# Raw attention scores stored with neighbouring queries interleaved in DRAM: wider fetches, split stores

## The chip, the cores and the metric

The kernel runs on one core of a Trainium2 chip. The core has five engines with a queue each: TensorE (PE for matmuls, PEld for the weight loads that run beside them), VectorE (DVE), ScalarE (ACT), GpSimd (POOL) and SyncE (SP, which here issues all transfers), and 16 DMA engines that move data between DRAM and the core's SBUF. The metric is the device time of one execution in microseconds, the median of several runs. All data are 32-bit floats.

## The reference

Attention with mixing over the heads before and after the softmax, followed by a gated layer without a nonlinearity:

```python
# q, k, v: [8 batches, 12 heads, 448, 64]; w_pre, w_post: [12, 12]
scores = scale * np.matmul(q, k.transpose(0, 1, 3, 2))
scores = np.einsum('bhij,hg->bgij', scores, w_pre)
scores = scores - np.max(scores, axis=-1, keepdims=True)
attn = np.exp(scores)
attn = attn / (np.sum(attn, axis=-1, keepdims=True) + 1e-09)
attn = np.einsum('bhij,hg->bgij', attn, w_post)
attn_out = np.matmul(attn, v)
...
x = attn_out.transpose(0, 2, 1, 3).reshape(8 * 448, 768)
h = (x @ w1) * (x @ w2) @ w3        # w1, w2: [768, 1024], w3: [1024, 1024]
return h @ w_out                    # [1024, 768]
```

## The kernel before

**Raw scores.** `qk` (L167) makes the raw scores of two heads (a head pair `p`) for a chunk `c` of 128 queries: eight matmuls into two PSUM tiles `psq` (one per head), two ScalarE copies into a stage tile `st` of 128 queries x 2 heads x 448 keys (L180, L181), and a store of `st` to the DRAM tensor `raw_d[b]` of 448 queries x 12 heads x 448 keys. The last chunk has 64 queries only, so two head pairs share its `st`, which leaves in two stores (L186); the others leave in one (L189). A batch has 21 such units: 18 of chunks 0 to 2 and three of chunk 3. `st` has two buffers per pool. The store is not issued at once: `qk` returns it, and the step loop puts it on the list `later` for the next step.

**Mixing over heads.** TensorE contracts over partitions, so for the mixing the heads must lie on partitions. `fetch` (L196) reads `raw_d` back by blocks of ten queries (45 blocks a batch, the last with eight): five queries x 12 heads are 60 rows, the two halves `s` of a block stand at partitions 0 and 64 of the tile `r`, and the two blocks `c` of a pair lie side by side along the free dimension. Two blocks of one batch and of full width come in two transfers, one per half (L203); other pairs (across two batches, or with the eight-query block) in four (L210). `r` has two buffers. `mix` (L215) multiplies by the pre-mixing weights into `psm` (L221); `largest` (L224) takes the maximum, `exp` (L231) the exponentials `e` and their sums, `scale` (L240) folds the reciprocal sums into the post-mixing weights `w2`, and `post` (L251) mixes again and transposes into the PSUM tiles `pso`. `put` (L273) copies `pso` into `mt` (L275; the eight-query block in two copies, L278), where the queries of a group of 15 blocks stand in order. `av` (L293) multiplies `mt` by `v` for a whole group.

**The gated layer** runs on TensorE between these parts as a background: first the product w3 @ w_out (L361), then batches 0 and 1 one by one (L523, L554), then the other six in pairs, in a scheme with seven products (L704). Its weights come in units `wu` from DRAM (L394); from batch 2 on the attention results pass through DRAM as `x_d` and are read back as `x` (L620).

**Order.** Everything is issued by a hand-written loop of steps (from L893 on, N = 360 blocks and six more); step `n` handles block pair `m = n // 2`, with different work in odd and even steps. In an even step SyncE gets first the fetch of the pair two ahead, which must wait until the mixing of the pair that held the buffer is done. Then come, by `do_later`, the weight units due, the list `later` (stores of raw scores and others), the operands `x`, and then the next `kq` (queries and keys of a head pair, L158). SyncE works through its queue in order: a transfer that waits holds up those behind it. The raw scores of batch 1 begin at step 11, beside those of batch 0; those of batch `b` > 1 are spread over the 45 steps before that batch's own blocks begin.

Of the kernel before, what the change touches and what calls it, by code (L numbers as in the profile page):

```python
# [6 lines left out]
F32 = mybir.dt.float32  # L7
# [8 lines left out]
B, H, S, D = 8, 12, 448, 64  # L16
DM, FF = 768, 1024
HP = H // 2
IB = 10
GI = H * IB  # L20
NB = -(-S // IB)
QT, NJ = 128, 4
GB = 15
NG = NB // GB
KF, K1 = FF // 128, DM // 128
IH = IB // 2
HK = H * IH
PP = 64
JB = S // PP
SETS = NB * B // 2  # L30
FIRST = 48
# [19 lines left out]
class Kernel:  # L51
# [115 lines left out]
    def qk(self, b, p, c, banks):  # L167


        nc = self.nc  # L170
        ps = [self.bank(i, f"psq{b}_{p}_{c}_{s}")[:, :S] for s, i in enumerate(banks)]
        for z, (t, q, k) in enumerate(self.parts(b, p, c)):
            for s in range(2):
                rows = slice(s * D, (s + 1) * D)
                nc.tensor.matmul(ps[s][z * PP:(z + 1) * PP], t[rows, q:q + PP], t[rows, k:k + S], start=True, stop=True)  # L175
        if b == c == 0:
            st = self.sz[:, 2 * p:2 * p + 2]
        else:
            st = (self.qp if b == 0 and p % 2 else self.kp).tile([128, 2, S], F32, tag="st", name=f"st{b}_{p}_{c}", bufs=2)
        nc.scalar.copy(st[:, 0], ps[0])  # L180
        (nc.vector.tensor_copy if b == c == 0 else nc.scalar.copy)(st[:, 1], ps[1])  # L181
        raw = self.raw_d[b]
        if c == 3:
            def store():
                for z in range(2):
                    nc.sync.dma_start(raw[3 * QT:, 2 * (p + z) - 2:2 * (p + z)], st[z * PP:(z + 1) * PP])  # L186
            return store
        n = QT if b or c else FIRST
        return lambda: nc.sync.dma_start(raw[c * QT:c * QT + n, 2 * p:2 * p + 2], st[:n])  # L189


# [4 lines left out]
    def fetch(self, m):  # L196
        r = self.rp.tile([128, 2, S], F32, tag="r", name=f"r{m}", bufs=2)
        self.rs[m] = r
        b, t = divmod(2 * m, NB)
        if t + 1 < NB and self.width(2 * m + 1) == IB:  # L200
            src = self.raw_d[b][t * IB:(t + 2) * IB].rearrange("(c s i) h j -> s (i h) c j", c=2, s=2)
            for s in range(2):
                self.nc.sync.dma_start(r[s * PP:s * PP + HK], src[s])  # L203
            return
        for c in range(2):
            b, t = divmod(2 * m + c, NB)
            for s in range(2):
                k = self.half(2 * m + c, s)
                src = self.raw_d[b][t * IB + s * IH:t * IB + s * IH + k].rearrange("i h j -> (i h) j")
                self.nc.sync.dma_start(r[s * PP:s * PP + H * k, c], src)  # L210

    def half(self, n, s):
        return min(IH, self.width(n) - s * IH)

    def mix(self, m):  # L215
        nc, r = self.nc, self.rs.pop(m)
# [34 lines left out]
    def post(self, m):  # L251
        nc, w2s = self.nc, self.w2s.pop(m)
        if any(b in (4, 5) for b, _ in self.ends):
            self.do_ends()
        for s, e in enumerate(self.es.pop(m)[0]):
            for j in range(JB):
                a, z = divmod(j, 2) if j < JB - 1 else (NJ - 1, s)
                at = (2 * a + s) * HK
                for c in range(2):
                    k = slice(c * PP, c * PP + HK)  # L260
                    nc.tensor.matmul(self.pso[c][z * PP:(z + 1) * PP, at:at + HK], e[k, j * PP:(j + 1) * PP], w2s[k, s],  # L261
                                     start=True, stop=True)
        for c in range(2):
            n = 2 * m + c
            w, (b, t) = self.width(n), divmod(n, NB)
            a, u = divmod(t, GB)
            if u == 0:
                self.mt[b, a] = self.mp.tile([128, NJ, H, GB * IB], F32, tag="mt", name=f"mt{b}_{a}")
            src = self.pso[c][:, :NJ * 2 * HK].rearrange("p (j s g i) -> p j s g i", j=NJ, s=2, g=H)
            dst = self.mt[b, a][:, :, :, u * IB:u * IB + w]  # L270
            self.ends.append((4 + c, lambda dst=dst, src=src, w=w: self.put(dst, src, w)))

    def put(self, dst, src, w):  # L273
        if w == IB:
            self.nc.scalar.copy(dst.rearrange("p j g (s i) -> p j s g i", s=2), src)  # L275
        else:
            for s, k in ((0, IH), (1, w - IH)):
                self.nc.scalar.copy(dst[:, :, :, s * IH:s * IH + k], src[:, :, s, :, :k])  # L278
# [465 lines left out]
    def run(self):  # L744
        nc, tc = self.nc, self.tc
# [5 lines left out]
        self.jobs, self.ys, self.pairs = [], {}, False  # L751
        dp = self.pool("dram", 1, space=DRAM)
        self.ps = self.pool("ps", 1, space=PSUM)
        self.raw_d = [dp.tile([S, H, S], F32, name=f"raw{b}_d") for b in range(B)]
        self.w_d = [dp.tile([KF, 128, k, 2, 128], F32, name=f"w{i}_d") for i, k in enumerate((K1, K1, KF))]
        self.x_d = [dp.tile([2, 128, K1 // 2, S], F32, name=f"x{b}_d") for b in range(B)]
        self.s_d = [{m: dp.tile([c, 128, k * 256], F32, name=f"s{i}_{m}_d") for m in (3, 5, 6, 7)}
# [22 lines left out]
        w = self.kp.tile([128, 2, S], F32, tag="st", name="wpre_s", bufs=2)[:, 0, :PP]  # L780
# [35 lines left out]
        for b in range(1, B):  # L816
            first, per = (11, 28 / 21) if b == 1 else ((b - 1) * NB - 6, NB / 21)
            units = [(b, p, c) for g in range(0, HP, 2) for p, c in [*itertools.product((g, g + 1), range(3)), (g + 1, 3)]]
            for i, (b, p, c) in enumerate(units):
                n = int(first + i * per) | (b > 1)  # L820
# [3 lines left out]
        for b in range(B):  # L824
            for a in range(NG):
                for g in range(HP):
                    n = (b * NB + (a + 1) * GB + 3) | 1
# [65 lines left out]
        for n in range(N + 6):  # L893
# [34 lines left out]
            m, odd = divmod(n, 2)  # L928
# [10 lines left out]
            p, pieces = self.n_made - 1 if fold_pieces else 2 * KF + 3 * KF, None  # L939
            if avs.get(n):  # L940
                pass
            elif fold_pieces:
                f = (self.n_made - 1 - 2 * KF) // 3
# [68 lines left out]
def words(w):  # L1012

    import numpy as np
    return np.ascontiguousarray(w).view(np.int64)


def layouts(inputs):
    import numpy as np
    q, k, v = inputs["q"], inputs["k"], inputs["v"]  # L1020
    qt = q.transpose(0, 1, 3, 2).reshape(B, HP, 2, D, S)
    kt = k.transpose(0, 1, 3, 2).reshape(B, HP, 2 * D, S)
    kq = np.ascontiguousarray(np.stack([qt.reshape(B, HP, 2 * D, S), kt], axis=3))
    q0 = qt[0].reshape(HP, 2 * D, S)
    kq0 = np.ascontiguousarray(np.concatenate([q0[:, :, :QT], kt[0], q0[:, :, QT:]], axis=2))
    vv = np.concatenate([v, v[:, :, (NJ - 1) * 128:]], axis=2)
    vv = vv.reshape(B, HP, 2, NJ, 128, D).transpose(0, 1, 4, 3, 2, 5).reshape(B, HP, 128, NJ, 128)
    wpre = np.zeros((128, PP), np.float32)
    wpost = np.zeros((128, HK), np.float32)
    for s in range(2):  # L1030
        for i in range(IH):
            rows = slice(s * PP + i * H, s * PP + (i + 1) * H)
            wpre[rows, i * H:(i + 1) * H] = inputs["w_pre"]
            wpost[rows, i::IH] = inputs["w_post"]
    return {
        "kq": kq, "kq0": kq0, "v": np.ascontiguousarray(vv), "wpre": wpre, "wpost": wpost,
        "w1": words(inputs["moe_w1"]), "w2": words(inputs["moe_w2"]),
        "w3t": words(inputs["moe_w3"].T), "wo": words(inputs["moe_w_out"]),
    }
# [16 lines left out]
```

## Time and profile before

| | |
|---|---|
| median of three runs | 1437.4 us (1436.35 to 1438.15) |
| the profiled execution | 1441.87 us, of which its span is 1439.9 us |
| TensorE busy | 1386.1 us (96%), weight loads 1056.7 us |
| ScalarE, VectorE, GpSimd busy | 833.3, 742.8, 622.0 us |
| read from DRAM, written to it | 279.77 MB, 134.09 MB |

The profile's page gives busy times, the span in 40 slices, the DMA queues, a chain of work followed back from the last instruction, the costliest groups of instructions (by line, engine, tiles and shape, with busy time, mean duration and what ended the idle time before them) and the DMA issues with their median time to landing. Further views tell who waited for whom, list instructions or transfers of a stretch of time, and tabulate busy times by stretches. A matmul's end is modelled, so a busy TensorE is not one at its peak.

### The profile page before, as it was taken

How to read it: one execution, taken by the hardware profiler on the slowest of the kernel's cores; microseconds unless marked ns; L12 is line 12 of the kernel's file. 1: busy time of each engine (PE TensorE's matmuls, PEld its weight loads, DVE VectorE, ACT ScalarE, POOL GpSimd, SP SyncE). 2: the span in 40 equal slices, each digit the busy share in tenths (PEclk: the TensorE clock that was granted, in tenths of full speed). 3: DMA queues.
4: the chain of work that ended last, by engine and by line, in shares of the span. 5: the costliest groups of instructions: out<-in, count | busy, mean ns of one | idle time of the engine just before them, and what ended most of it. 6: DMA issues, size and time to landing. Idle time of an engine off the chain costs nothing.

```text
span 1439.9 us, 45779 instructions
## 1 busy us (share of the span) xinstructions
PE 1386.1 (96%) x18684; PEld 1056.7 (73%) x18684; DVE 742.8 (52%) x1497; ACT 833.3 (58%) x1952; POOL 622.0 (43%) x754
## 2 busy tenths in 40 slices
PE   5879999999999999999999999999999999999998
PEld 2357786766677767776777777777777777889988
DVE  5957566767644545432344435334444456345563
ACT  4866666767756756665655556556556445432231
POOL 1423233444324544532345345434335436457693
PEclk8989999999999999999999999999999999999999
DMA  8998789999999999999889988799979757698775
GB/s 283 366 319 277 237 266 321 325 312 305 313 280 356 368 357 318 380 348 333 286 266 290 315 289 265 247 316 332 300 229 301 248 174 224 196 327 268 239 234 171
DMA packets 203761, 416.87 MB, mean 290 GB/s; under 512 B 20528, under 2 KB 120112, under 8 KB 203472
## 3 DMA queue, kind: packets, MB, share of 16 engines
q1 hardware_dynamic: 203552, 413.94, 87.5%
q8 instruction: 149, 2.44, 0.7%
q14 instruction: 60, 0.49, 0.1%
HBM read 279.77 MB, written 134.09 MB: 287 GB/s over the span
## 4 chain that ended last, share of the span: by engine, by line
PE 81%; DMA 9%; DVE 5%; ACT 2%; issue 1%; SPq 0%; POOL 0%; DVEq 0%; POOLq 0%; ACTq 0%
PE e L704 20%; PE psa L302 11%; PE pso L261 10%; PE psm L221 8%; PE psq L175 7%; PE eg L523 6%; PE psf L361 4%; PE eo L554 4%; PE e2o L704 4%; PE e3o L704 4%; DMA wu<-w_d 3%; PE e1o L704 3%; DMA raw_d<-st 2%; DMA cs<-wo 2%; DMA r<-raw_d 1%
## 5 line engine op out<-in xcount | busy, mean ns | idle before, releaser
L248 POOL TENSOR_SCALAR w<-wpo,ri 128x60 f32<-128x60 f32 x360 | 180.3, 517 | 482.9 <-DVE ri L246 464.6
L228 DVE TENSOR_REDUCE mn<-psm 128x1 f32<-128x448 f32 x360 | 207.6, 618 | 319.1 <-PE psm L221 318.8
L275 ACT COPY mt<-pso 128x480 f32<-128x480 f32 x352 | 197.8, 621 | 183.6 <-PE pso L261 183.4
L704 PE MATMUL e<-eh,wu 128*128 128x448 f32 x1008 | 297.3, 371 | 4.4 <-DVE c L658 3.2
L236 ACT ACTIVATE e<-psm,mn 128x448 f32<-128x448 f32 x360 | 226.8, 643 | 8.3 <-DVE mn L228 8.3
L704 PEld LDWEIGHTS e<-eh,wu 128*128 128x128 f32 x1008 | 187.5, 188 | 50.9 <-issue 25.1
L221 PE MATMUL psm<-r,wsc 60*64 60x448 f32 (+1 forms) x1440 | 193.1, 552 | 20.7 <-DVE cx L124 7.8
L261 PEld LDWEIGHTS pso<-w,e 60*64 60x64 f32 x10080 | 175.3, 135 | 50.9 <-issue 42.2
L261 PE MATMUL pso<-w,e 60*64 60x60 f32 x10080 | 199.2, 224 | 0.4 <-ACT mt L275 0.3
L704 PE MATMUL e<-el,wu 128*128 128x448 f32 x504 | 186.8, 371 | 0.0
L302 PE MATMUL psa<-mt,v 128*64 128x150 f32 (+1 forms) x2304 | 158.5, 294 | 4.2 <-ACT st L180 4.2
L302 PEld LDWEIGHTS psa<-mt,v 128*64 128x64 f32 x2304 | 145.1, 138 | 20.3 <-ACT st L180 6.9
L175 PE MATMUL psq<-kq 64*64 64x448 f32 x1176 | 156.1, 542 | 4.0 <-ACT st L180 4.0
L658 DVE TENSOR_TENSOR c<-c,e 128x448 f32<-128x448 f32 x168 | 101.6, 617 | 82.5 <-PE e L704 77.9
L180 ACT COPY st<-psq 128x448 f32<-128x448 f32 x162 | 86.5, 534 | 79.7 <-ACT mt L275 34.1
L523 PE MATMUL eg<-xh,wu 128*128 128x448 f32 x384 | 118.8, 380 | 3.3 <-DMA wu<-w_d 3.3
L643 POOL TENSOR_TENSOR el<-x,eh 128x448 fp32r<-128x448 f32 x90 | 104.2, 1174 | 34.4 <-ACT eh L642 28.9
L704 PEld LDWEIGHTS e<-el,wu 128*128 128x128 f32 x504 | 94.6, 188 | 22.2 <-issue 14.1
L175 PEld LDWEIGHTS psq<-kq 64*64 64x64 f32 x1176 | 60.7, 135 | 58.1 <-issue 30.0
L523 PEld LDWEIGHTS eg<-xh,wu 128*128 128x128 f32 x384 | 71.4, 189 | 36.0 <-issue 24.7
L245 DVE TENSOR_SCALAR sa<-sm 128x2 f32<-128x2 f32 x180 | 35.2, 196 | 116.0 <-ACT e L236 115.6
L181 ACT COPY st<-psq 128x448 f32<-128x448 f32 x162 | 87.8, 542 | 0.0
(99 smaller groups left out, 2015.6 us busy)
## 6 DMA issues: line engine op xcount, KB each, us to landing
r<-raw_d SPq DMA_DIRECT2D x344, 210.0 KB, 5.4
raw_d<-st SPq DMA_DIRECT2D x138, 448.0 KB, 6.2
wu<-w_d SPq DMA_DIRECT2D x104, 384.0 KB, 6.4
wu<-s_d SPq DMA_DIRECT2D x96, 384.0 KB, 4.9
wu<-w_d SPq DMA_DIRECT2D x51, 512.0 KB, 6.2
kq<-kq SPq DMA_DIRECT2D x42, 448.0 KB, 7.1
wu<-s_d SPq DMA_DIRECT2D x36, 512.0 KB, 5.0
x<-x_d SPq DMA_DIRECT2D x72, 224.0 KB, 6.4
```

What stands on the lines that cost most here:

```text
L175: nc.tensor.matmul(ps[s][z * PP:(z + 1) * PP], t[rows, q:q + PP], t[rows, k:k + S], start=True, stop=True)
L221: nc.tensor.matmul(ps[s][c * PP:(c + 1) * PP, :S], self.wsc[k], r[k, c], start=True, stop=True)
L228: self.nc.vector.tensor_reduce(mn[:, s:s + 1], self.psm[m][s][:, :S], axis=AX.X, op=ALU.min)
L236: nc.scalar.activation(e, p[:, :S], AF.Exp, bias=mn[:, s:s + 1], scale=-1.0, accum_out=sm[:, s:s + 1])
L248: nc.gpsimd.tensor_scalar_mul(w2[:, s], self.wpo, ri[:, s:s + 1])
L261: nc.tensor.matmul(self.pso[c][z * PP:(z + 1) * PP, at:at + HK], e[k, j * PP:(j + 1) * PP], w2s[k, s], start=True, stop=True)
L275: self.nc.scalar.copy(dst.rearrange("p j g (s i) -> p j s g i", s=2), src)
L302: nc.tensor.matmul(self.psa[rows, g % 3, :W], v[:, j, rows], mt[:, j, 2 * g + s, :W], start=(j == 0), stop=(j == NJ - 1))
L523: nc.tensor.matmul(p, u[:, k % (K1 // 2), x], xs[y][:, k], start=(k == 0 and t == 0), stop=(k == K1 - 1 and t == 2))
L643: nc.gpsimd.tensor_tensor(lo, x, hi.bitcast(F32), op=ALU.subtract)
L658: nc.vector.tensor_tensor(a[out], a[to[0]], p, op=ALU.add)
L704: nc.tensor.matmul(p, w[:, k, x], ops[m, k][y], start=(k == 0 and t == 0), stop=(k == nk - 1 and t == 2))
```

## The change

For batches 1 to 7 `raw_d[b]` becomes a tensor of 224 query pairs x 12 heads x 2 x 448 keys: for each head the scores of queries 2i and 2i + 1 are neighbours. On the host the queries of each chunk are reordered, even ones first, so that partitions 0 to 63 of `st` hold the even queries of a chunk and 64 to 127 the odd ones. Each `st` leaves in two stores of 64 partitions (chunk 3: four of 32), each with two runs of 448 numbers per partition. A pair of full blocks of one group of 15 is fetched in two transfers whose 60 rows are one run of 896 numbers each; `c` is now the parity of the query and `s` the half of the twenty. Pairs that cross a group, a batch or meet the eight-query block come in four transfers, with `s` as the parity. `put` writes with a step of two so that `mt` has the queries in order as before. Batch 0 stays as it is.

```diff
@@ qk
         raw = self.raw_d[b]
+        if b:
+            n, parts = (PP // 2, ((2 * p - 2, 0), (2 * p, PP))) if c == 3 else (PP, ((2 * p, 0),))
+
+            def store():
+                for h, k in parts:
+                    for z in range(2):
+                        nc.sync.dma_start(raw[c * PP:c * PP + n, h:h + 2, z], st[k + z * n:k + (z + 1) * n])
+            return store
...
-        n = QT if b or c else FIRST
+        n = QT if c else FIRST
@@ fetch
         b, t = divmod(2 * m, NB)
-        if t + 1 < NB and self.width(2 * m + 1) == IB:
+        if self.paired(2 * m):
+            src = self.raw_d[b][t * IH:(t + 2) * IH].rearrange("(s i) h c j -> s (i h) c j", s=2)
+            for s in range(2):
+                self.nc.sync.dma_start(r[s * PP:s * PP + HK], src[s])
+            return
+        if b == 0 and t + 1 < NB and self.width(2 * m + 1) == IB:
...
-                src = self.raw_d[b][t * IB + s * IH:t * IB + s * IH + k].rearrange("i h j -> (i h) j")
+                raw = self.raw_d[b][t * IH:t * IH + k, :, s] if b else self.raw_d[b][t * IB + s * IH:t * IB + s * IH + k]
+                src = raw.rearrange("i h j -> (i h) j")
                 self.nc.sync.dma_start(r[s * PP:s * PP + H * k, c], src)
 
     def half(self, n, s):
-        return min(IH, self.width(n) - s * IH)
+        return min(IH, self.width(n) - s * IH) if n < NB else self.width(n) // 2
+
+    def paired(self, n):
+
+        t, u = n % NB, (n ^ 1) % NB
+        return n >= NB and n // NB == (n ^ 1) // NB and t // GB == u // GB and self.width(n) == self.width(n ^ 1) == IB
@@ post
-            dst = self.mt[b, a][:, :, :, u * IB:u * IB + w]
-            self.ends.append((4 + c, lambda dst=dst, src=src, w=w: self.put(dst, src, w)))
-
-    def put(self, dst, src, w):
-        if w == IB:
+            if b == 0:
+                dst = self.mt[b, a][:, :, :, u * IB:u * IB + w]
+            elif self.paired(n):
+                dst = self.mt[b, a][:, :, :, (u - c) * IB:(u - c + 2) * IB].rearrange("p j g (s i c) -> p c j s g i", s=2, c=2)[:, c]
+            else:
+                src = src[:, :, :, :, :w // 2]
+                dst = self.mt[b, a][:, :, :, u * IB:u * IB + w].rearrange("p j g (i s) -> p j s g i", s=2)
+            self.ends.append((4 + c, lambda dst=dst, src=src, w=w, b=b: self.put(dst, src, w, b)))
+
+    def put(self, dst, src, w, b):
+        if b:
+            self.nc.scalar.copy(dst, src)
+        elif w == IB:
             self.nc.scalar.copy(dst.rearrange("p j g (s i) -> p j s g i", s=2), src)
@@ run
-        self.raw_d = [dp.tile([S, H, S], F32, name=f"raw{b}_d") for b in range(B)]
+        self.raw_d = [dp.tile([S // 2, H, 2, S] if b else [S, H, S], F32, name=f"raw{b}_d") for b in range(B)]
@@ layouts
-    kq = np.ascontiguousarray(np.stack([qt.reshape(B, HP, 2 * D, S), kt], axis=3))
+    order = [c + 2 * i + z for c, n in ((0, QT), (QT, QT), (2 * QT, QT), (3 * QT, PP)) for z in range(2) for i in range(n // 2)]
+    kq = np.ascontiguousarray(np.stack([qt.reshape(B, HP, 2 * D, S)[..., order], kt], axis=3))
```

## Prediction

> **What bounds the kernel now.** I read the page first, then the table of stretches, the waits of TensorE, the chain in the stretch with the most idle time, and last the two queues of work that the change touches: SyncE's issues and the stage copies of ScalarE. From the page:
>
> ```profile
> PE 1386.1 (96%) x18684; PEld 1056.7 (73%) x18684; DVE 742.8 (52%) x1497; ACT 833.3 (58%) x1952; POOL 622.0 (43%) x754
> ...
> DMA  8998789999999999999889988799979757698775
> ...
> DMA packets 203761, 416.87 MB, mean 290 GB/s; under 512 B 20528, under 2 KB 120112, under 8 KB 203472
> ...
> q1 hardware_dynamic: 203552, 413.94, 87.5%
> ```
>
> TensorE is busy 1386.1 of 1439.9 us, so no change to transfers can win more than the other 53.8 us. But the DMA engines are almost as full. The table of stretches (us, then PE, PEld, DVE, ACT and POOL busy with counts, the granted clock, DMA share, GB/s) says where:
>
> ```profile
> 40.00:100.00 60.00, 43.94 (x631) 24.67 (x633) 46.33 (x90) 44.76 (x108) 22.45 (x28) 0.92 1.02 362
> ...
> 240.00:300.00 60.00, 58.92 (x937) 41.55 (x937) 44.50 (x94) 46.69 (x112) 26.40 (x35) 1.00 0.99 334
> ...
> 420.00:720.00 300.00, 293.63 (x4475) 216.94 (x4473) 131.75 (x281) 191.50 (x454) 124.63 (x154) 0.98 1.00 341
> 720.00:960.00 240.00, 239.72 (x3446) 183.86 (x3448) 106.47 (x233) 145.01 (x342) 109.87 (x141) 1.00 0.88 281
> 960.00:1020.00 60.00, 58.84 (x889) 44.32 (x885) 21.80 (x50) 36.48 (x85) 21.93 (x30) 1.00 1.02 341
> ```
>
> In four stretches, 480 us together, the DMA engines are full (share 0.99 to 1.02). In three of these TensorE still works nearly all the time: 1.1 us are lost from 240 to 300, 6.4 from 420 to 720, 1.2 from 960 to 1020. Only from 40 to 100 us are 16.1 us lost. So after the first 100 us the transfers are hidden, with little to spare. What TensorE waited for, first from 40 to 100 us, then from 100 us to the end (us, times, longest):
>
> ```profile
> PE psq L175 <- ACT st L180: 9.8, 7, 3.3
> PE psa L302 <- ACT st L180: 2.3, 1, 2.3
> ```
> ```profile
> PE psm L221 <- ACT e L236: 5.2, 8, 1.4
> PE psm L221 <- DMA r<-raw_d: 3.5, 2, 2.4
> PE eg L523 <- DMA wu<-w_d: 3.3, 3, 2.0
> ...
> PE psa L302 <- ACT st L180: 1.9, 3, 0.7
> ```
>
> After 100 us waits on transfers that the change could shorten come to 3.5 + 3.3 = 6.8 us: that is about all a lighter DMA load can bring. Before 100 us the loss goes through the stage copy `st`, and the chain in that stretch (start, us, what) shows what holds it:
>
> ```profile
> 72.95 7.95 DMA raw_d<-st
> ...
> 80.98 0.53 ACT st L180
> ...
> 89.43 7.32 DMA raw_d<-st
> ...
> 96.82 0.54 ACT st L180
> ...
> 97.41 2.82 PE psa L302 x21
> ```
>
> `st` has two buffers, and a copy waits until the store two units before has landed. By the order of units (batch 1 starts at step 11, beside the end of batch 0), the stores at 72.95 and 89.43 are chunk 0 of head pairs 0 and 1 of batch 1: stores that the change splits.
>
> **Part 1: the fetches (L198 to L210).** Per block pair and half the fetch moves 60 rows of two runs of 1,792 bytes; afterwards 60 runs of 3,584 bytes, the same 210 KB. A pair that crosses a group of 15 blocks is now fetched in four transfers of 105 KB in place of two: once per batch 1 to 7, 14 transfers more. In batches 1 to 7, 150 pairs are fetched whole now, 143 afterwards. Packets: 150 x 240 = 36,000 become 143 x 120 + 7 x 240 = 18,840, so 17,160 fewer.
>
> **Part 2: the stores (L182 to L189).** Per batch 18 stores of 448 KB (128 rows of one 3,584-byte run) become 36 of 224 KB (64 rows of two 1,792-byte runs); three pairs of 224 KB become three times four of 112 KB. Over seven batches: 126 + 42 = 168 transfers more, and 126 x 128 + 21 x 128 = 18,816 packets more.
>
> Parts 1 and 2 move the same bytes; net there are 1,656 packets more, 0.8% of 203,761. The queue's mean packet took 0.875 x 16 x 1439.9 / 203,552 = 99 ns, payload included. At that price the net is 1,656 x 99 / 16 = 10 us of each DMA engine's time, an upper bound. The lower one is not zero: were shorter read packets dear and shorter write packets free, the fetches alone would save up to 17,160 x 99 / 16 = 106 us of DMA time; the reverse would add 116 us. No row separates reads from writes, the two nearly cancel, and I take 0, and keep both signs for the rivals. At 0 the full stretches stay as full as they are.
>
> **Part 3: SyncE.** It issues all of these in one order. The rows of the raw tensor (duration ns min/median/max) price an issue, and its waits show what slack there is (whole run, then the stretch from 420 to 720 us):
>
> ```profile
> L203 SPq DMA_DIRECT2D r<-raw_d x344: 315/399/1800, 15.5 to 1227.0; - x172
> L189 SPq DMA_DIRECT2D raw_d<-st x138: 319/343/1640, 29.5 to 1077.8; - x138
> L186 SPq DMA_DIRECT2D raw_d<-st x48: 451/587/1188, 75.1 to 1083.6; - x48
> L210 SPq DMA_DIRECT2D r<-raw_d x32: 290/391/1276, 185.9 to 1233.8; - x32
> ```
> ```profile
> SPq L203 <- PE psm L221: 296.3, 107, 6.5
> ...
> SPq L203 <- DMA wu<-w_d: 9.9, 15, 1.3
> ```
> ```profile
> SPq L203 <- PE psm L221: 40.0, 18, 5.3
> ```
>
> The 64-partition store of L186 is the nearest form, dearer to issue (587 ns) than the 128-partition one (343). So 126 x (2 x 587 - 343) = 105 us, 21 x 2 x 587 = 25 us, and 7 x (4 x 391 - 2 x 399) = 5 us: 135 us more on SyncE, about 0.83 us behind each ordinary store. Behind it in the queue stand the split operands `x`, the next `kq`, and the fetch of the next step. That fetch is the cover: SyncE comes to it early and waits 296.3 us in 107 places for the mixing matmuls to free `r`. So I cost it at 0. Where the cover is thin, from 420 to 720 us, 300 of the 1010 us from the first split store (72.95) to the last (1083.6), the share is 300 / 1010 x 135 = 40 us against 40.0; but there SyncE also waits for landings that have nothing to do with the transfer it holds (a fetch for weights `wu`, 9.9 us), so the number of transfers under way is limited, and issue time hides behind these waits too. If this cover is gone, each store pushes the next fetch by 0.83 us.
>
> **Part 4: when `st` comes free.** Now one landing frees it, then two. Lightly loaded, the trace has both forms side by side: the issues of a pair of 64-partition stores (start, us), and the median time to landing of the issues from 105 to 111 us:
>
> ```profile
> 105.92 1.09 SPq L186 DMA_DIRECT2D raw_d<-st  x2
> ```
> ```profile
> raw_d<-st SPq DMA_DIRECT2D x2, 224.0 KB, 2.9
> raw_d<-st SPq DMA_DIRECT2D x1, 448.0 KB, 2.7
> ```
>
> The second half is issued 0.54 us after the first, so the pair is down after 0.54 + 2.9 = 3.4 us against 2.7: 0.7 us later, the upper bound in an ordinary state. In a full queue bytes decide, and they are the same: 0 is the lower bound, and a gain is excluded, since the second half is issued behind the first. The chain's two stores stand in a full stretch; between 0 and 0.7 I take 0.25 us for each, nearer to the full state: +0.5 us. Later the copies still wait for stores, the whole run against 40 to 100 us:
>
> ```profile
> ACT st L180 <- DMA raw_d<-st: 16.2, 10, 3.6
> ```
> ```profile
> ACT st L180 <- DMA raw_d<-st: 11.8, 6, 3.6
> ```
>
> That leaves 4 waits (4.4 us) after or before it; 4 x 0.25 = 1 us, of which I let 0.4 reach TensorE, whose own waits on `st` after 100 us are only 1.9 us.
>
> [...]
>
> **Part 5: ScalarE's copy to `mt` (L275).** It now writes every second element. No row has a strided write; the nearest is a strided read (L111 takes every second word) beside a plain one of that length:
>
> ```profile
> L275 ACT COPY mt<-pso 128x480 f32<-128x480 f32 x352 | 197.8, 621 | 183.6 <-PE pso L261 183.4
> ...
> L111 ACT ACTIVATE cm<-cs 128x384 f32<-128x384 f32 x64 | 36.3, 568 | 15.1 <-DVE cx L125 8.7 <-DMA cs<-wo 6.3
> ...
> L130 ACT CAST wu<-cx 128x384 fp32r<-128x384 f32 x32 | 16.9, 527 | 0.0
> ```
>
> That is 568 - 527 = 41 ns per 384 elements, about 50 ns for 480; over 308 copies between 0 and 15 us on an engine that is 58% busy and waited 183.4 us for TensorE just before these copies. A gain is excluded, as nothing gets shorter. I take 0. The matmuls, the reordering of queries on the host and the last block's halves (4 and 4 rows in place of 5 and 3) cost nothing on the path.
>
> Sum: 0 + 0 + 0.5 + 0.4 + 0 = +0.9 us. The profiled execution took 1441.87 us (span 1439.9 and 2.0 around it); it becomes 1442.8. It lies 4.5 us over the median of the three runs, 1437.4, so I predict 1438.3. About 0.2% (2.9 us) is what a measurement of this kernel can tell from no change; +0.9 lies within it.
>
> **Rivals.**
> *The lighter reads shorten the full stretches.* If a longer read run saves more than a shorter write run costs, `r` and `wu` land earlier where DMA is full. A third of the 106 us, 35 us, of which 447 / 1010 (the full stretches from 73 us on) is 15 us, would already outrun waits that are at most 2.4 us long. For it: DMA share 1.0 there. Against it: only 6.8 us are to be had, and the writes take back as much as they can. It gives 1437.4 - 6.8 = 1430.6 at best, 1432.5 in the middle.
> *`st` comes free too late.* Mechanism: two landings before the copy. It decides when the second landing trails by over about 0.4 us and a tenth or more of the 147 copies have less slack than that. Price: two chain links and 15 copies at 0.7 us, half of the latter on TensorE: 1.4 + 5.2 = +6.6 us, 1444; 1441 to 1448 with fewer or more. For it: the chain from 60 to 100 us. Against it: only 4 waits outside that stretch now.
> *SyncE falls behind in the full stretch.* 40 us of issues against 40.0 of cover from 420 to 720 us; if some ten fetches there come 0.83 us later and TensorE waits for each: +8 us, 1446.
> [...]
> *The change does not do what it says*: the 896 numbers still go out as two runs. Then 18,816 packets are only added, at most 116 x 447 / 1010 = 51 us in full stretches, of which a tenth to a third may reach TensorE: 1442 to 1454.
>
> **How the numbers follow.** No measurable change 0.48 (its own range 1435.5 to 1440.3), lighter reads 0.22, late `st` 0.17, SyncE 0.06, half rate 0.04, unmerged runs 0.03. Faster 0.22, same 0.48, slower 0.30. The range 1431.5 to 1448 leaves out the best of the second case, half rate, and the far ends of the last ones, some 0.16 together.
>
> **What would show it.** Right: about 1,656 packets more and the same MB; DMA share still near 1.0 in the four stretches; 64-partition stores at 450 to 590 ns an issue; SyncE's wait for `psm` down by about 100 us without TensorE's waits on `r` rising; L275 at 621 to 670 ns; the two `st` links of the chain longer by less than 0.7 us each. Wrong: waits on `r` or `wu` gone and DMA share down (reads were dear), waits on `st` doubled, or packets up by far more than 1,656.

## The result and the profile after

The changed kernel took 1455.52 us (median of six runs, 1449.91 to 1463.38), the kernel before beside it 1438.76: a ratio of 1.0133 [1.0114, 1.0152]. By the medians it is 16.8 us slower, by the ratio 19.1 us; the forecast was 1438.3 with a range up to 1448. The profiled execution after is the slowest of the six, 1463.38 us with a span of 1461.6, that is 21.7 us more span than in the profile before. One disturbed run of an experiment (1536.8 us, stores split by heads) and one of the kernel before (4607.8 us) are left out of the ratios below.

The page of the kernel after (busy times, then packets):

```profile
PE 1395.1 (95%) x18684; PEld 1062.0 (73%) x18684; DVE 743.1 (51%) x1497; ACT 847.0 (58%) x1945; POOL 623.1 (43%) x754
...
DMA packets 208352, 416.90 MB, mean 285 GB/s; under 512 B 23461, under 2 KB 126357, under 8 KB 208061
...
q1 hardware_dynamic: 208141, 413.95, 88.0%
```

The same bytes moved, in 4,591 packets more. TensorE was busy 9.0 us longer and idle 12.7 us longer. The table of stretches, with the columns of before:

```profile
40.00:100.00 60.00, 44.22 (x631) 25.00 (x633) 46.33 (x90) 43.92 (x105) 22.11 (x28) 0.89 1.01 349
240.00:300.00 60.00, 58.40 (x925) 40.96 (x920) 43.79 (x93) 47.44 (x111) 26.17 (x35) 1.00 0.99 325
420.00:720.00 300.00, 282.90 (x4238) 207.45 (x4228) 124.82 (x264) 185.95 (x428) 118.52 (x145) 0.97 0.98 327
...
960.00:1020.00 60.00, 58.85 (x875) 45.16 (x873) 22.82 (x53) 37.44 (x88) 23.33 (x33) 1.00 0.99 317
```

From 40 to 100 us, where the chain ran through `st`, nothing is lost. In the full stretch from 420 to 720 us TensorE is busy 10.7 us less, and the transfers move 327 GB/s in place of 341, at a DMA share of 0.98 in place of 1.00: the DMA engines did not get busier. Matched by the starts of the mixing matmuls, the kernel after is within 1 us of before until 451 us, 7.1 us late at 514, 16.6 at 692, 17.0 at 947 and 22.3 at 1133. What TensorE waited for after 100 us (total us, times, longest), with the columns of the prediction:

```profile
PE eg L550 <- DMA wu<-w_d: 9.0, 6, 2.8
PE psm L240 <- DMA r<-raw_d: 6.4, 2, 3.5
...
PE e L731 <- DMA wu<-w_d: 2.1, 1, 2.1
PE psa L329 <- ACT st L180: 1.9, 3, 0.7
```

The waits on `r` rose from 3.5 to 6.4 us and those on the weights `wu` from 3.8 (3.3 and 0.5) to 11.1; those on `st` are as before. The first 100 us are left out because a stall of some 8 us at the first mixing stands there in both kernels, and the profile puts it down to different causes (before, then after):

```profile
18.74 1.83 PE L221 MATMUL psm<-r,wsc 60*64 60x448 f32 x5 [7.79 <-DVE cx L124]
```
```profile
18.28 1.96 PE L240 MATMUL psm<-r,wsc 60*64 60x448 f32 x5 [7.91 <-DMA r<-raw_d]
```

What SyncE's fetches waited for, the whole run, and then from 420 to 720 us:

```profile
SPq L211 <- PE psm L240: 183.5, 77, 6.8
...
SPq L216 <- PE psm L240: 17.0, 9, 5.0
...
SPq L224 <- PE psm L240: 9.5, 4, 3.7
```
```profile
SPq L211 <- PE psm L240: 15.7, 11, 3.7
```

L216 holds batch 0's fetches, which before stood in L203 with the others. All fetches together waited 301.6 us for a free `r` before (L203 and 5.3 us of L210) and 210.0 after; in the full stretch it was 40.0 and 15.7. This wait is what the prediction called the cover. The issues of the raw scores (ns min/median/max):

```profile
L189 SPq DMA_DIRECT2D raw_d<-st x336: 302/581/2398, 72.1 to 1103.6; - x168
L211 SPq DMA_DIRECT2D r<-raw_d x286: 315/393/3092, 192.5 to 1249.2; - x143
L224 SPq DMA_DIRECT2D r<-raw_d x60: 314/404/1857, 185.3 to 1255.9; - x60
```

Summed over all of SyncE's issue records, issuing took 607 us before (1,292 transfers) and 779 us after (1,474). One stall in the chain of waits (start, us, what):

```profile
617.72 5.99 DMA r<-raw_d
...
623.77 5.38 DMA s_d<-s
...
629.21 11.01 DMA r<-raw_d
...
640.36 2.06 PE psm L240 x8
642.42 1.49 PE psq L175 x8
```

It is a chain of landings, linked by SyncE: the fetch issued at 629.21 is held until an unrelated store `s_d` has landed, which itself was held by another landing. In the trace all of SyncE's 1,474 transfers take eight semaphores in turn, none is issued before the transfer eight before it has landed (the 1,283 of these landings that are recorded in full), and at most eight are under way. The last hold was short (0.4 us). The fetch then took 11.0 us to land, where the same fetch before took 6.5 and landed before its matmuls were due; why it took so long is not shown. TensorE has no work from 637.4 to 640.4 us, and works slower behind it: stretches of 2 us around the stall (the granted clock is the third number from the end) show

```profile
638.00:640.00 2.00, 0.00 (x0) 0.00 (x0) 0.00 (x0) 0.62 (x2) 0.00 (x0) 0.80 0.90 352
640.00:642.00 2.00, 1.64 (x9) 1.22 (x13) 0.00 (x0) 0.00 (x0) 0.00 (x0) 0.50 0.89 330
642.00:644.00 2.00, 2.00 (x13) 0.53 (x5) 1.16 (x2) 0.01 (x1) 0.00 (x0) 0.50 0.99 360
644.00:646.00 2.00, 2.00 (x6) 1.78 (x7) 0.00 (x0) 2.00 (x6) 0.00 (x0) 0.50 0.92 262
646.00:648.00 2.00, 2.00 (x29) 1.59 (x31) 0.34 (x2) 0.73 (x3) 0.84 (x2) 0.99 0.78 237
```

nothing done until 640, then half the clock until 646. From 620 to 645 us a mixing matmul took 542 ns (median), and up to 1003 at half the clock. After 100 us the clock records hold 13.7 us at half speed before and 27.3 after; half of the difference, an estimate, is some 7 of the 9 us of busy time added. After 100 us these windows are 3.41 or 6.83 us long, and in the kernel after TensorE was busy for 0.7 to 1.8 of the 3.4 us before each of them. What sets the clock down is not shown. The added half-clock time belongs to this execution, the slowest of the six: two kernels below lose as much with 13.7 us (split into halves) and 10.2 us (plain copy) at half speed.

### The profile page after: what moved, and what is told of

Its sections match the earlier page's. It is cut to its first block, busy times and chain, and to the rows that moved or that the text cites. A ratio compares the mean times of both kernels' runs of the same rounds, so it can differ in the third digit from the quotient of the medians.

```text
span 1461.6 us, 46041 instructions
## 1 busy us (share of the span) xinstructions
PE 1395.1 (95%) x18684; PEld 1062.0 (73%) x18684; DVE 743.1 (51%) x1497; ACT 847.0 (58%) x1945; POOL 623.1 (43%) x754
## 4 chain that ended last, share of the span: by engine, by line
PE 74%; DMA 15%; DVE 5%; ACT 2%; issue 1%; SPq 1%; POOL 0%; DVEq 0%; ACTq 0%; POOLq 0%
PE e L731 20%; PE psa L329 10%; PE pso L280 9%; PE psm L240 8%; PE psq L175 6%; PE psf L388 4%; PE eg L550 4%; DMA r<-raw_d 4%; PE e2o L731 4%; PE e3o L731 4%; PE eo L581 3%; PE e1o L731 3%; DMA wu<-w_d 2%; DMA raw_d<-st 2%; DMA v<-v 2%
## 5 line engine op out<-in xcount | busy, mean ns | idle before, releaser
L300 ACT COPY mt<-pso 128x480 f32<-128x480 f32 x315 | 190.7, 672 | 177.9 <-PE pso L280 177.6
L255 ACT ACTIVATE e<-psm,mn 128x448 f32<-128x448 f32 x360 | 227.4, 645 | 6.9 <-DVE mn L247 6.5
L240 PE MATMUL psm<-r,wsc 60*64 60x448 f32 (+1 forms) x1440 | 199.5, 558 | 25.1 <-DMA r<-raw_d 15.6
L175 PE MATMUL psq<-kq 64*64 64x448 f32 x1176 | 160.5, 546 | 3.7 <-ACT st L180 3.7
```

The source lines that it names most:

```text
L240: nc.tensor.matmul(ps[s][c * PP:(c + 1) * PP, :S], self.wsc[k], r[k, c], start=True, stop=True)
L255: nc.scalar.activation(e, p[:, :S], AF.Exp, bias=mn[:, s:s + 1], scale=-1.0, accum_out=sm[:, s:s + 1])
L300: self.nc.scalar.copy(dst, src)
```

## The experiments

The theories, by the letters of the expectations. A: the number of transfers under way is limited, and smaller ones fill it with fewer bytes. B: SyncE's time for issuing falls behind. C: the shorter write runs cost DMA time. D: the strided copy to `mt`. F: `st` comes free too late. Each ratio is against the kernel before, run on the same chip beside it.

**Is it the split, and does the layout matter?** Four kernels take the change apart. Stores split by heads (two of 128 partitions, 1,792 bytes each), in the kernel before:

```diff
+        if b:
+            def store():
+                for h in range(2):
+                    nc.sync.dma_start(raw[c * QT:(c + 1) * QT, 2 * p + h], st[:, h])
+            return store
```

> The kernel before, with the stores of batches 1 to 7 split by heads: two transfers of 128 partitions and one run of 1,792 bytes each (chunk 3: four of 64 partitions). 168 transfers and 18,816 packets more, as in the change, but issued at about 340 ns each; the fetch and the layout stay. Theory A (the number of transfers under way is limited, so more and smaller ones keep fewer bytes moving): about as slow as the change, +10 to +20 us over before. Theory B (SyncE's 580 ns for each 64-partition store): only some 60 us more on SyncE, so 0 to +5 us. Theory C (shorter write runs cost DMA time): +10 to +20 us. Theory D (strided copy on ScalarE): no change.

Measured 1.0097 [1.0062, 1.0132]: 14 us, more than the 0 to 5 us that B expected. Stores split into partition halves, again in the kernel before, so that runs and packets of data stay as they were:

```diff
...
+                for k in range(0, QT, PP):
+                    nc.sync.dma_start(raw[c * QT + k:c * QT + k + PP, 2 * p:2 * p + 2], st[k:k + PP])
```

> The kernel before, with the stores of batches 1 to 7 split by partitions: two transfers of 64 partitions with one run of 3,584 bytes each (chunk 3: four of 32). 168 transfers more as in the change, no packets more, issued at 450 to 590 ns each; fetch and layout stay. Theory A: +10 to +20 us. Theory B: +10 to +20 us. Theory C: 0 to +4 us. Theory D: no change.

Measured 1.0147 [1.0122, 1.0171]: the whole loss, with the old layout, the old fetches and no shorter run. C is not needed, and the 18,816 packets more of the split by heads did not make it dearer than this one. The long reads alone, in the kernel before (each row takes 896 contiguous numbers of the unchanged tensor, so other scores are mixed than the reference's):

```diff
+            if b:
+                src = self.raw_d[b][t * IB:(t + 2) * IB].rearrange("(s i) (h c) j -> s (i h) c j", s=2, c=2)
```

> The kernel before, with stores as they were, and the paired fetches of batches 1 to 7 reading 60 rows of one run of 3,584 bytes from the unchanged layout: the rows are then other scores than the reference mixes, of the same number. No transfer more, 18,000 packets fewer. Theories A and B: -4 to +1 us against before, the gain that lighter reads can bring. Theory C, reversed for reads (a long run is served no faster): 0. If long reads were what hurts: +10 us or more.

Measured 1.0003 [0.9986, 1.0019]. Its page:

```profile
DMA packets 185761, 416.87 MB, mean 290 GB/s; under 512 B 20528, under 2 KB 84112, under 8 KB 185472
```

18,000 packets fewer buy nothing. The change with the copy to `mt` of before (the queries of a group then stand in another order):

```diff
-        if b:
-            self.nc.scalar.copy(dst, src)
-        elif w == IB:
+        if w == IB:
```

> The changed kernel, with the copy to mt as in the kernel before (no step of two; the queries of a group then stand in another order than the reference's). Theories A, B and C: as slow as the change, 1450 to 1458 us, at most 3 us faster through 16 us less on ScalarE. Theory D: back to 1438 to 1442 us.

Measured 1.0145 [1.0123, 1.0167]: no better than the change, so D falls.

**Transfers without bytes.** The kernel before with a 240-byte transfer behind each store of batches 1 to 7, 168 in all, and with two of them:

```diff
                 nc.sync.dma_start(raw[c * QT:(c + 1) * QT, 2 * p:2 * p + 2], st)
+                self.tiny()          # tiny_d[k] <- wpo[:1], 240 bytes
...
```

> The kernel before, with a transfer of 240 bytes (from the constant weights to a scratch tensor in DRAM) issued behind each store of batches 1 to 7, two behind those of chunk 3: 168 transfers more as in the change, without bytes, without a second landing for st and without 64-partition stores. Theory A (each transfer takes one of a fixed number of places, whatever its size): +6 to +15 us. Theory B (SyncE's issue time; here some 0.3 us each, 50 us in all, against 170 us in the change): 0 to +5 us. Theory F (st comes free late, two landings): 0.

> The kernel before, with two transfers of 240 bytes behind each store of batches 1 to 7 (four behind chunk 3's): 336 transfers more, some 95 us more on SyncE, no bytes. Theory A: twice the loss of one tiny transfer (+9.6 us), so +16 to +24 us. Theory B: between that and, if the empty instructions cost as much, the same as they.

Measured 1.0067 [1.0051, 1.0083] with one and 1.0229 [1.0192, 1.0265] with two: 9.6 us as A expected, then 32.9 us, more than the 16 to 24 of A. No second landing holds `st` here, so F is not needed. With two, the issues, the full stretch, and TensorE's waits after 100 us:

```profile
L202 SPq DMA_DIRECT2D tiny_d<-wpo x336: 212/269/1133, 73.8 to 1114.5; - x168
```
```profile
420.00:720.00 300.00, 278.70 (x4162) 203.81 (x4162) 124.09 (x264) 179.76 (x427) 118.18 (x146) 0.97 0.97 324
```
```profile
PE psm L232 <- DMA r<-raw_d: 12.6, 5, 6.1
PE eg L534 <- DMA wu<-w_d: 10.5, 6, 3.8
```

80 KB of added data cost more than the whole change, in the same place and by the same waits.

**SyncE's time without transfers.** The kernel before with 16, and later 28, empty SyncE instructions behind each of these stores:

```diff
+                for _ in range(16):
+                    nc.sync.nop(hint="x", nofuse=True)
```

> The kernel before, with 16 empty instructions on SyncE behind each store of batches 1 to 7 (32 behind those of chunk 3's 42): time on SyncE alone, without a transfer. Their duration is to be read from the profile; at 20 to 60 ns each they add 50 to 160 us to SyncE, about what the change adds (170 us). Theory B (SyncE's issue time): +8 to +20 us if they come to 100 us or more. Theory A (places for transfers under way): 0 to +3 us.

> The kernel before, with 28 empty SyncE instructions behind each store of raw scores of batches 1 to 7 (168 times) in place of the 16 of the run before; no transfer is added. The 16 took 0.56 to 0.66 us, 102.5 us in all, and cost 0.49%. 28 should take about 1.0 us, 170 to 180 us in all, which is what the change itself adds to SyncE's issue time (779 us against 607). Theory A (the limited number of transfers under way): SyncE's time alone is only part of the loss, so this stays well below 1.0133: by the line through the run with 16, 1.008, with 1.005 to 1.010 allowed. Theory B (SyncE's issue time is all of it): the full loss of the change, 1.013, with 1.011 to 1.016 allowed.

The empty instructions do not show in the profile's views, but as gaps in SyncE's timeline (start, us); with 28, about 1.1 us behind each store:

```profile
641.22 0.34 SPq L193 DMA_DIRECT2D raw_d<-st  x1
642.64 0.34 SPq L402 DMA_DIRECT2D wu<-w_d  x1
...
646.15 0.34 SPq L193 DMA_DIRECT2D raw_d<-st  x1
647.57 0.34 SPq L402 DMA_DIRECT2D wu<-w_d  x1
```

By their records the groups take 102.5 us in all with 16 and 181.8 with 28. The issue records took 28 us less than before in both (579 us), so SyncE's time rose by 74 and 153 us net. Measured 1.0049 [1.003, 1.0069] and 1.0102 [1.0085, 1.0118]. Both lie between what the theories expected (for 28: A 1.008, B 1.013): SyncE's time alone, in about the size of the change (172 us), makes some three quarters of its loss, and not clearly all of it. Full stretch and SyncE's wait there, with 28:

```profile
420.00:720.00 300.00, 287.80 (x4318) 212.03 (x4314) 127.52 (x271) 186.49 (x441) 122.05 (x149) 0.97 0.98 333
```
```profile
SPq L211 <- PE psm L229: 32.7, 17, 4.6
```

About 50 us of empty instructions fall into this stretch. The wait for a free `r` gave up 7 us for them (32.7 left of 40.0), and the waits for a place some 34 (next table). So the added time did find idle time of SyncE to go into, and TensorE still worked 5.8 us less.

**The queue of the full stretch.** The issue and landing records from 420 to 720 us, worked out for four kernels ("under way": mean number between the end of an issue and its landing; "place": SyncE idle until the landing eight transfers before):

| | issued | MB | under way | of them tiny | issue, us | waits for a place, us | GB/s |
|---|---|---|---|---|---|---|---|
| before | 323 | 102.3 | 6.42 | 0 | 160 | 69 | 341 |
| after | 357 | 98.0 | 6.46 | 0 | 203 | 55 | 327 |
| two tiny | 401 | 97.3 | 6.36 | 1.04 | 171 | 97 | 324 |
| 28 empty | 313 | 99.8 | 6.05 | 0 | 153 | 35 | 333 |

With empty instructions fewer transfers are under way, of the same size (319 KB each, 317 before). After the change as many are under way as before, but each is smaller (274 KB). A expects this, and the landing times fit; before and after, from 420 to 720 us (KB each, median us to landing):

```profile
r<-raw_d SPq DMA_DIRECT2D x88, 210.0 KB, 6.6
raw_d<-st SPq DMA_DIRECT2D x36, 448.0 KB, 6.6
```
```profile
r<-raw_d SPq DMA_DIRECT2D x80, 210.0 KB, 6.0
raw_d<-st SPq DMA_DIRECT2D x70, 224.0 KB, 5.9
```

A store of half the bytes holds its place nearly as long (5.9 us against 6.6). The rate falls although most transfers land sooner. The table alone does not show that the places cause the loss: while TensorE stands still less is asked for, and of the 4% that the rate fell only 1.4 points are idle DMA engines (share 0.996 to 0.982); the rest is that a MB took 48.1 us of their time in place of 46.7. With two tiny transfers it took 47.7, with the data's packets unchanged.

**Other queues.** The change with its split stores issued by ScalarE, which here shares SyncE's places:

```diff
-                        nc.sync.dma_start(raw[c * PP:c * PP + n, h:h + 2, z], st[k + z * n:k + (z + 1) * n])
+                        nc.scalar.dma_start(raw[c * PP:c * PP + n, h:h + 2, z], st[k + z * n:k + (z + 1) * n])
```

> The changed kernel, with its 336 split stores issued by ScalarE in place of SyncE. SyncE is rid of 200 us of issues; the places for transfers under way are shared between the two engines as this program is built. Theory B: back towards before, at most +5 us, if ScalarE can bear some 200 us of issues. Theory A: still +10 us or more; ScalarE's load may add to that.

Measured 1.0757 [1.0735, 1.0778]. ScalarE's queue now waits for landings of SyncE's transfers too (in front of the exponentials of L255 9.6 us for `r` and 8.2 for `kq`, which they do not read; none of either in the change). TensorE waits for the exponentials, since ScalarE stands behind its own stores:

```profile
PE psm L240 <- ACT e L255: 61.0, 39, 9.1
```

The same with GpSimd (`nc.gpsimd`) issuing the 336 split stores of the change, and the unsplit stores of before on GpSimd:

> [...] Theories A and B: the loss is gone, -8 to +4 us against before, unless GpSimd's issues hold up its own work (w2, the low parts): then slower, with TensorE waiting for GpSimd and not for r or wu. Theory F: still +8 us or more.

> The kernel before, with its stores of batches 1 to 7 (168, unsplit) issued by GpSimd. If places and SyncE's queue limit the full stretches already before the change: -3 to -10 us. If GpSimd's issues are in the way: 0 to +10 us, with waits for GpSimd.

Measured 1.0094 [1.0076, 1.0111] and 1.0049 [1.0033, 1.0065]. For the split stores A and B both expected the loss to be gone; it was 13.5 us, though SyncE and its places were relieved of all 336 (that GpSimd's transfers take none of SyncE's places is read from the loads of `kq` below). The unsplit stores cost half a per cent on GpSimd, and the split adds about as much. GpSimd's busy time rises with its issues, to 719.4 us unsplit and 818.3 split, in place of 622.0:

```profile
PE 1389.9 (96%) x18684; PEld 1059.0 (73%) x18684; DVE 777.1 (54%) x1497; ACT 847.0 (58%) x1945; POOL 818.3 (56%) x1090
```

But TensorE waited for GpSimd at most 2.4 us in any row of the split version, and after 100 us 5.8 us for `r` and 6.1 for `wu`. F expected 8 us or more, but TensorE's waits on `st` are 13.3 us there and 14.0 before. What makes the split dear on GpSimd is not shown.

Then 84 other transfers (the loads of `kq`, and of `v` for batches 1 to 7) moved to GpSimd instead, in the kernel before and in the change:

```diff
-        self.nc.sync.dma_start(t, self.kq[b, p].rearrange("p a j -> p (a j)"))
+        self.nc.gpsimd.dma_start(t, self.kq[b, p].rearrange("p a j -> p (a j)"))
...
-        self.nc.sync.dma_start(t, self.v[b, g])
+        (self.nc.gpsimd if b else self.nc.sync).dma_start(t, self.v[b, g])
```

> The kernel before, with the loads of kq and of v for batches 1 to 7 (84) issued by GpSimd, which has places of its own: 84 transfers fewer in SyncE's queue and its places. Theory A: -2 to -6 us, since the full stretches are limited by places already before the change. Theory B: -1 to -3 us (84 x 0.4 = 34 us less on SyncE). If neither limits before the change: 0, or +1 to +4 us through GpSimd's issues of some 0.55 us.

> The changed kernel, with the loads of kq and of v for batches 1 to 7 issued by GpSimd. Half of the 168 added transfers are thus taken out of SyncE's places. Theory A: about half of the loss is gone, +5 to +11 us over before instead of +19. Theory B: 34 us of the 170 us gone, +14 to +17 us.

Measured 0.9992 [0.9977, 1.0008] and 1.0113 [1.0086, 1.014]. From 420 to 720 us SyncE waited 8.4 us for landings of `kq` in the change; with `kq` on GpSimd no such row of over 0.8 us is left. For the kernel before it changed nothing that can be told (-1.1 us, from -3.3 to +1.1). For the change the loss was 16.2 us (12.3 to 20.1): not the 5 to 11 us that A expected with half the added transfers out of SyncE's places, but within B's 14 to 17. Its interval reaches the 1.0133 of the change.

**The layout without the split.** Heads outermost in DRAM, so that neighbouring queries of a head are neighbours and one store of 128 partitions does:

```diff
-                        nc.sync.dma_start(raw[c * PP:c * PP + n, h:h + 2, z], st[k + z * n:k + (z + 1) * n])
+                    nc.sync.dma_start(raw[h:h + 2].rearrange("h i z j -> (i z) h j")[c * QT:c * QT + n], st[k:k + n])
...
@@ fetch
+                src = self.raw_d[b][:, (t + s) * IH:(t + s + 1) * IH].rearrange("h i c j -> i h (c j)")
```

> The change without its split: the raw scores of batches 1 to 7 lie with the head as the outer index, so that neighbouring queries of one head are neighbours in DRAM too. The fetches read the same 60 runs of 896 numbers as in the change, the write runs are as short (two runs of 448 numbers per partition), and the copies to mt write with a step of two; but a stage tile leaves in one store of 128 partitions as before (two of 64 for the last chunk), and the queries need no reordering. Only the 14 transfers of the pairs across a group of blocks come on top of before. Theories A and B (number of transfers, or SyncE's time on them): both are as before, so the loss is gone, 1.000, with 0.998 to 1.003 allowed. Theory C (short write runs cost DMA time): the loss stays, 1.010 to 1.015. If the long reads are worth anything when nothing else changes: below 0.998.

Measured 1.1695 [1.1672, 1.1719], which no theory expected, and it has another cause. The 60 rows of a fetch are now 5 queries by 12 heads with two strides. In a light stretch, 205 to 235 us, in 40 slices:

```profile
DMA  9999973333339999999999438936988367996369
GB/s 290 296 351 385 389 244 145 124 139 124 122 133 379 388 358 296 320 225 296 297 380 410 193 138 316 354 143 219 325 340 356 119 141 223 325 339 221 132 189 258
```
```profile
L210 SPq DMA_DIRECT2D r<-raw_d x286: 710/720/1517, 189.8 to 1466.3; - x143
```

For over 4 us the DMA share is three tenths, at 122 to 145 GB/s, but the kernel before has such a stretch too (0.38 at 124 GB/s from 211 to 216 us). The full stretch tells more: from 420 to 720 us the share is 0.78 at 260 GB/s, in place of 1.00 and 341. Over the run TensorE waited 88.0 us for `r`, in place of 5.5, and the fetches, the stores of `st` and the loads of `wu` waited 194.4 us in SyncE's queue for landings of `r`, in place of 12.4. What makes these fetches slow is not shown. As they are what TensorE waits for most, this run says nothing about the split.

**The change, stored by heads.** Its layout, transfers and packets, but 128 partitions a store:

```diff
-                        nc.sync.dma_start(raw[c * PP:c * PP + n, h:h + 2, z], st[k + z * n:k + (z + 1) * n])
+                        nc.sync.dma_start(raw[c * PP:c * PP + n // 2, h + z], st[k:k + n, z])
```

> The change with each stage tile stored by heads in place of by even and odd queries: two stores of 128 partitions, one run of 448 numbers each (the last chunk four of 64 partitions). The layout in DRAM, the fetches, the number of transfers and the packets are those of the change; the queries need no reordering. Only the issue should be cheaper: 319 ns in the run that stored by heads in the old layout, against 581 ns for 64 partitions in the change, so about 126 x 2 x 0.26 = 66 us less on SyncE. If SyncE's time is the main part of the loss, as the run with 28 empty instructions has it (182 us cost 1.02%), 66 us less takes back some 0.37%: 1.010, with 1.007 to 1.0115 allowed. If the number of transfers is the main part: the loss stays, 1.013, with 1.0115 to 1.016 allowed.

Measured 1.0095 [1.0073, 1.0117], in the range expected of B, but not by the means assumed:

```profile
L189 SPq DMA_DIRECT2D raw_d<-st x336: 512/552/1702, 72.8 to 1092.6; - x168
```

The issue costs 552 ns, not 319; and 319 was the shortest issue of the run by heads in the old layout, whose median was 382. All issues together took 751 us, 28 less than in the change, where 66 were expected; at 0.53% per 79 us (from 16 to 28 empty instructions) that explains some 0.2 of the 0.38 points, and the intervals of this kernel and the change still touch. In the old layout the two splits (1.0147 and 1.0097) differ by 53 us of issue time, worth 0.36 of their 0.50 points at that price. Whether 64 partitions cost something besides stays open. It is hardly their time to landing: from 420 to 720 us the stores of 224 KB land in 5.6 and 5.7 us (median) with 128 partitions, and in 5.7 and 5.9 with 64.

**What follows.** Splitting the stores is enough for the whole loss: the halves in the old layout, with the old fetches, cost 1.47%. Layout, long reads, short writes and the strided copy are not needed for it. The added transfers cost in two ways. One is SyncE's time (0.49% for 74 us net, 1.02% for 153). The other goes with the number of transfers, which A puts down to the places: two tiny transfers per store add 71 us of issue records, no more than the 16 empty instructions on the same chip, and cost 2.29%. That each costs by itself is shown. How the 1.33% divides stays open: issue time of about the change's size is worth up to three quarters of it, but 1.02% and the 0.67% of one tiny transfer per store together exceed the whole, so the two do not simply add. Taking 84 other transfers out of SyncE's places won back less than A expected. Where SyncE issues everything, TensorE's waits on `r` and `wu` after 100 us, each from one execution, go with the loss (heads first left out):

| kernel | ratio | waits on `r` and `wu`, us |
|---|---|---|
| before | 1 | 7.3 |
| long reads | 1.0003 | 9.9 |
| 16 empty | 1.0049 | 9.7 |
| one tiny | 1.0067 | 12.5 |
| change, stored by heads | 1.0095 | 14.6 |
| before, split by heads | 1.0097 | 13.9 |
| 28 empty | 1.0102 | 13.8 |
| change | 1.0133 | 17.5 |
| change, plain copy | 1.0145 | 15.7 |
| before, split into halves | 1.0147 | 20.4 |
| two tiny | 1.0229 | 26.7 |

No version was measurably faster than the kernel before.

## Why the prediction was wrong

**The step that failed is Part 3**, in its words: "So I cost it at 0." The path it named is the one that lost the time, SyncE's issues where the cover is thin, from 420 to 720 us; the term was mis-sized in two ways.

First, the cover. The issue time was close (135 us forecast, 172 measured), and the fetches' wait for `psm` did fall by about the 100 us named (301.6 to 210.0). But the sum of the waits is no cover where it is thin. From 420 to 720 us 40 us were set against 40.0; there SyncE's issues took 43 us more (160 to 203), of which 24 came from the waits for `r` and some 15 from the waits for a place, and TensorE still lost 10.7 us. The 40.0 us stood in 18 steps of up to 5.3 us, and cover in one step does not serve the next: after the change 15.7 us of it were left over, with 28 empty instructions 32.7.

Second, the places. The prediction saw that the number of transfers under way is limited, and took those waits as one more cover ("issue time hides behind these waits too"). They are not free: with 28 empty instructions some 34 us of them were used up in the stretch, fewer transfers were under way (6.05 in place of 6.42), and 1.02% was lost. It also left the 182 added transfers out of the count of places: the same 6.4 under way with 274 KB each in place of 317 hold 14% less. The tiny transfers show that added transfers cost without bytes; how much of the change's loss this is was not shown.

The rival *SyncE falls behind in the full stretch* had the right place and mechanism, at 0.06 and +8 us. It looked for the loss at the fetches alone. TensorE's waits on `r` rose by 2.9 us after 100 us, those on `wu` by 7.3.

**Parts 1 and 2** were right in their net of about zero, and the bounds of 106 and 116 us were far too wide: long reads are worth nothing that shows (1.0003 with 18,000 packets fewer), and short writes none either (1.0097 by heads, 1.0147 into halves without them). The packets rose by 4,591 and not by 1,656: under 512 B the page counts 2,933 more, about 16 for each of the 182 transfers, and the trace's packets of 1,792 and 3,584 bytes rise by the 1,656. **Part 4** came out near its sum: from 40 to 100 us TensorE's busy time is 44.22 us against 43.94, and its waits on `st` over the whole run are 13.6 us against 14.0. That is partly luck, since two of its reasons did not hold. The chain's two stores land 1.1 and 0.4 us earlier than before, a gain that it had excluded:

```profile
73.08 6.71 DMA raw_d<-st
...
90.35 6.02 DMA raw_d<-st
```

And in the full queue bytes do not decide alone (5.9 us for half the bytes against 6.6). **Part 5** was right: this is the copy's row after, 51 ns over the 621 of before and off the path (1.0145 without the stride).

```profile
L300 ACT COPY mt<-pso 128x480 f32<-128x480 f32 x315 | 190.7, 672 | 177.9 <-PE pso L280 177.6
```

*Lighter reads* fell with the run of long reads, *unmerged runs* with the change's own packet count. *Late `st`* fell with TensorE's waits on `st`, which did not rise. A *half rate* for 64 partitions in full stretches, to which the chances give 0.04, is shown by no run: from 420 to 720 us stores of 64 partitions landed in 5.7 and 5.9 us (median), those of 128 with the same bytes in 5.6 and 5.7.

## What to carry to other kernels

Where DMA is full (share 1.00 here) and one queue issues everything, count transfers as well as bytes: a split that moves the same bytes costs one more issue and one more place each time (168 of them 1.47% here, into halves), in the very stretch where neither is free. Compare a queue's added time with its slack step by step in the tightest stretch, not with the sum of its waits over the run, and do not count its waits for a place as slack. Before reading a wait as the effect of a change, look whether the same stall stands in the profile before under another name, as the first 8 us here did.

## What the runs showed of the hardware

- A 240-byte transfer held a place for long: with two tiny per store, 94 of them from 420 to 720 us held 1.04 places on average, 3.3 us each. The cost grew faster than their number: 0.67% for 168, 2.29% for 336.
- An issue of two times 64 partitions by 3,584 bytes in the old layout (into halves) took 534 ns each (median), one of 128 partitions by 1,792 bytes (by heads) 382, and one of 128 partitions with the two-stride pattern of the change (stored by heads) 552. At the same bytes the issue's time differed with the access pattern.
- A run of 28 empty SyncE instructions takes about 1.1 us (181.8 us for 168 runs), 39 ns each; with 16 it is 38 ns each (102.5 us).
- Fetches of 5 queries by 12 heads with two strides (heads first) went with a DMA share of 0.78 at 260 GB/s from 420 to 720 us, and with 88.0 us of TensorE waiting for `r`; their issue took 720 ns (median) in place of 393 in the change, and the kernel 17% longer than before.
